# Block attention and a squared-ReLU FFN on one core: two turns fewer on TensorE, four sums in place of five, shared reciprocals, and an order of tasks that is written down

## The chip, the core and the metric

The kernel runs on one core of a Trainium2 chip. The core has TensorE (PE, the matmul engine, with its weight loads as PEld), VectorE (DVE), ScalarE (ACT), GpSimd (POOL) and SyncE (SP, which issues nearly all DMAs); they work side by side, each takes its own instructions strictly in order, and semaphores tie them together. The metric is the device time of one execution in microseconds, the median of several runs. A profile shows one further execution, whose span is a little shorter than a run's time.

## The reference, cut to what matters

Four batches of 768 tokens with eight heads of 64 go through local attention, and the 3072 tokens that come out through an FFN with weights of 512 x 2048 and 2048 x 512. All is in float32.

```python
k_sum = k.reshape(B, H, nb, 32, D).max(axis=3)        # nb = 24 block keys
v_sum = v.reshape(B, H, nb, 32, D).mean(axis=3)
scores_l = where(|i - j| < 16, scale * q @ k.T, -1e9)
scores_s = scale * q @ k_sum.T + log(32)
a = exp(concat - max);  a = a / (sum(a) + 1e-9)
x = a @ concat(v, v_sum)                              # to (3072, 512)
out = (max(x @ w_in, 0) ** 2) @ w_out
```

## The kernel before

**Tasks and queues.** The program is built from some 2400 named tasks. Each has an engine, a cost, a key (when it is due), the tasks it comes after, and the buffers it takes and uses. `Plan.order` (lines 234 to 355) is a planner that goes through time with these costs and keys and yields one list; the order of a task on its engine is its place in that list. Keys are moved by hand in a table `NUDGE`, and the first loads on SP are in a list `FIRST`.

**Attention.** The tokens are 48 groups of 64, taken in pairs. A group g has these tasks: QL, LV, LS load queries, values and block sums; KL, KM load keys (four blocks for each batch) and take their block maxima on DVE; KC and KW make copies of keys; S is the scores on PE, 16 matmuls in two halves, a second sixteen at the start adding the mask by PE (groups below `PE_MASKS = 8`; the scores' maximum is then X on DVE, line 945), while from group 8 on DVE masks and takes the maximum in M and Mb (line 913); E is four exponentials on ACT with their sums (line 976, one per pair of heads); R is the reciprocal on DVE (`inverse`, lines 988 to 995: an add with an accumulated by-product, then the reciprocal); N normalises, on DVE or on ACT (`NORMAL_BY`); T turns the weights. If `TURN_BY` gives a pair to PE, T is four transposes by PE and A a copy on ACT; if it gives it to DVE, T is a transpose by DVE within 32 x 32 squares, TW stores the pair to memory and TR_0 to TR_3 fetch it back in the turned layout, all on SP's queue. V is the visit: the pair's products with the values on PE, next to the scores of a later pair. XH and XL split the result into a high and a low part. All matmuls of the FFN are three products of such parts.

**FFN.** A unit is 512 tokens. Units 0 and 1 run plainly: for each of 16 slices f, FI (12 matmuls of 128 x 512, into the hidden slice), RL, SQ and GH on ACT, GL on DVE, FO (12 matmuls back; for f = 0 and 1 of unit 0 both come in halves a and b, FO in halves of six). Weights for it are loaded by WL, and split by WM and WH on ACT and WR, WJ and WW on DVE: the FFN's task FI0_f needs WH and WW of weight 0 and slice f (from f = 3 on both weights share a task, WW3). The remaining 2048 tokens are two super-units s, each of four blocks, multiplied in the seven-product scheme: `mixed` (lines 1777 to 1968) does the seven products with w_in, eight hidden blocks p at a time (SP tasks on PE, 56 per s), `products` (lines 1539 to 1667) the seven with w_out (FP, 56 per s), product j over its eight p after another. The sums of the weights (RC, SC, SH, SL, WS, and with i for w_in) are done on DVE and ACT meanwhile.

**The sums of the second products.** For every p four squared hidden parts `first`, `second`, `diff`, `last` are there. Of the seven left factors, five take a DVE addition of 128 x 512: TA1 and TB1 in `mixed` (lines 1884 to 1891 and 1937, 1938), and one each for j = 2, 5 and 6 (TA, lines 1578 to 1599). GH on ACT (line 1601) and GL on DVE (line 1605) then split the factor, and FP multiplies it with a loaded chunk of the weights (CL). A product runs in a bank of `o` over its eight p; after the eighth, U1 (ACT, line 1647), C11, U2, U3, C22, C21, C12 (DVE) take the banks out.

**Dummies.** Y tasks (`warm`, line 555) are pairs of dummy matmuls on PE that fill the start, 16 before the first scores and 8 more behind them.

## Time and profile before

| | |
|---|---|
| median of 3 runs | 567.49 us (567.41 to 567.75) |
| span of the profiled execution | 566.3 us |
| instructions in it | 11867 |
| PE busy | 557.6 us, 98% |
| weight loads busy | 459.4 us, 81% |
| DVE busy | 470.2 us, 83% |
| ACT busy | 373.9 us, 66% |
| POOL busy | 36.7 us, 6% |

The profile is read from the whole to the place: the totals of the engines, the chain of work that ended last (each step followed back to what released it), the waits of one engine by what released them, the chain or an engine's instructions in order of time, and the instructions grouped by line. Busy times of neighbours on one engine can overlap, since instructions are pipelined; the distance between two starts is then what one of them costs.

### The profile page before, as it was taken

To read this page: it belongs to the slowest core of one execution; us is meant where nothing else is said; L and a number is where in the kernel's file an instruction comes from. 1 tells how busy PE (TensorE), PEld (TensorE's weight loads), DVE (VectorE), ACT (ScalarE), POOL (GpSimd) and SP (SyncE) were. 2 spreads that over 40 slices of the span, in tenths; PEclk is the share of its full clock that TensorE was granted. 3 is DMA by queue.
4 is the path that set the end of the run, shared out by engine and by line. 5 is a ranking of instruction groups with operands and counts; after the bars stand their busy time and mean duration, and the time that the engine had idled before them with its cause. 6 is when DMAs were issued, how large, how long until landed. Compare 5 with 4: busy or idle time off the path is not lost.

```text
span 566.3 us, 11867 instructions
## 1 busy us (share of the span) xinstructions
PE 557.6 (98%) x3955; PEld 459.4 (81%) x3955; DVE 470.2 (83%) x1191; ACT 373.9 (66%) x968; POOL 36.7 (6%) x88
## 2 busy tenths in 40 slices
PE   8899999999999999999999999999999999999997
PEld 8688888888888888888888888888888888888885
DVE  4999999988799998999978889997493556868864
ACT  3899899878877987786336688847374532554442
POOL 4300000012001130000000200000000000000000
PEclk9999999999999999999999999999999999999999
DMA  8998999999989999899877989897975666767672
GB/s 314 354 371 306 364 328 383 290 289 370 341 272 323 322 341 371 301 293 393 298 211 236 292 247 284 274 281 239 281 224 159 194 190 194 193 197 230 191 234 96
DMA packets 86953, 156.75 MB, mean 277 GB/s; under 512 B 9011, under 2 KB 30837, under 8 KB 86893
## 3 DMA queue, kind: packets, MB, share of 16 engines
q1 hardware_dynamic: 85741, 152.95, 82.8%
q0 software_dynamic: 1152, 3.05, 3.2%
q8 instruction: 32, 0.52, 0.4%
q14 instruction: 28, 0.23, 0.1%
HBM read 111.66 MB, written 47.94 MB: 282 GB/s over the span
## 4 chain that ended last, share of the span: by engine, by line
PE 95%; ACT 2%; DVE 2%; issue 0%; POOL 0%; DVEq 0%; POOLq 0%; ACTq 0%
PE o L1620 23%; PE o L1322 16%; PE h L1296 15%; PE o L1844 14%; PE sz L1844 8%; PE att L1620 4%; PE x L1099 4%; PE att L840 3%; PE sa L1844 3%; PE att L1844 2%; PE warm L559 2%; ACT qvpa_lent L978 1%; PE t L1028 1%; DVE small L933 0%; PE o L840 0%; PE h_1a L1296 0%
## 5 line engine op out<-in xcount | busy, mean ns | idle before, releaser
L1602 ACT CAST gh<-g 128x512 fp32r<-128x512 f32 x112 | 69.2, 621 | 53.1 <-PE o L1620 22.7
L1620 PE MATMUL o<-gh,w 128*128 128x512 f32 x384 | 103.2, 391 | 0.0
L1607 DVE TENSOR_TENSOR gl<-g,gh 128x512 fp32r<-128x512 f32 x112 | 76.0, 685 | 21.1 <-ACT gh L1602 20.0
L1620 PEld LDWEIGHTS o<-gh,w 128*128 128x128 f32 x384 | 71.7, 188 | 14.9
L1296 PE MATMUL h<-xh,w 128*128 128x512 f32 x240 | 74.5, 391 | 0.0
L1881 ACT ACTIVATE g<-g 128x512 f32<-128x512 f32 x60 | 37.8, 632 | 49.4 <-DVE g L1877 49.3
L1322 PE MATMUL o<-w,gh 128*128 128x512 f32 x240 | 62.3, 395 | 0.0
L978 ACT ACTIVATE p<-p,small 128x118 f32<-128x118 f32 x160 | 61.8, 391 | 0.7 <-DVE small L915 0.7
L1620 PE MATMUL o<-gl,w 128*128 128x512 f32 x192 | 59.2, 389 | 0.0
L1296 PEld LDWEIGHTS h<-xh,w 128*128 128x128 f32 x240 | 44.7, 188 | 9.5 <-ACT rl_0b L1305 0.3
L1322 PEld LDWEIGHTS o<-w,gh 128*128 128x128 f32 x240 | 44.1, 188 | 9.4 <-ACT rl L1306 0.2
L1296 PE MATMUL h<-xl,w 128*128 128x512 f32 x120 | 46.7, 389 | 0.0
L1620 PEld LDWEIGHTS o<-gl,w 128*128 128x128 f32 x192 | 36.0, 188 | 7.6
L1844 PE MATMUL o<-w,w 128*128 128x512 f32 x160 | 40.5, 389 | 0.0
L1844 PEld LDWEIGHTS o<-w,w 128*128 128x128 f32 x160 | 30.0, 188 | 6.2
L915 DVE CUSTOM_DVE_ANT_0 p<-att,mask 128x118 f32<-128x118 f32 x152 | 32.9, 274 | 2.1 <-PE att L840 2.0
L1844 PE MATMUL sz<-xh,w 128*128 128x512 f32 x128 | 34.3, 390 | 0.0
L1322 PE MATMUL o<-w,gl 128*128 128x512 f32 x120 | 33.6, 389 | 0.0
L1597 DVE TENSOR_TENSOR g<-g 128x512 f32<-128x512 f32 x48 | 32.6, 684 | 0.2
L1877 DVE CUSTOM_DVE_ANT_0 g<-sz,g 128x512 f32<-128x512 f32 x32 | 22.0, 687 | 12.0 <-ACT g L1864 6.9
L978 ACT ACTIVATION_READ_ACCUMULATOR p<-p,small 128x1 f32 x160 | 31.2, 195 | 0.0
L1844 PE MATMUL o<-xh,w 128*128 128x512 f32 x112 | 30.1, 390 | 0.0
(197 smaller groups left out, 1093.9 us busy)
## 6 DMA issues: line engine op xcount, KB each, us to landing
raw<-wW SPq DMA_DIRECT2D x32, 512.0 KB, 7.7
w<-scr_t SPq DMA_DIRECT2D x64, 256.0 KB, 3.0
w<-scr_s SPq DMA_DIRECT2D x64, 256.0 KB, 3.0
w<-scr_a SPq DMA_DIRECT2D x48, 256.0 KB, 3.3
w<-scr_i SPq DMA_DIRECT2D x44, 256.0 KB, 3.1
turn<-a SPq DMA_DIRECT2D x17, 512.0 KB, 4.7
scr_t<-ci SPq DMA_DIRECT2D x16, 512.0 KB, 8.1
v<-vS SPq DMA_DIRECT2D x34, 192.0 KB, 3.5
```

The lines of the kernel that those rows point to most:

```text
L915: nc.vector.tensor_tensor_reduce(out=pr.tile[:, j, :KEYS], in0=score_at(g, 0, j), in1=mask_of(g)[0], scale=-SCALE, scalar=-NEG, op0=ALU.ad ...
L978: nc.scalar.activation(x, score_tile(g, p % parts)[:, p] if by_pe else x, AF.Exp, bias=nm.tile[:, p : p + 1], scale=SCALE if by_pe else -1 ...
L1099: nc.tensor.matmul(x_of(i)[h % 2 * D : (h % 2 + 1) * D, h // 2, :], lhsT=v_bufs[g].tile[:KEYS, h * D : (h + 1) * D], rhs=av[:KEYS, 2 * c : ...
L1296: nc.tensor.matmul(cut(h), lhsT=lhs.tile[:, k // 2, k % 2 * P : (k % 2 + 1) * P], rhs=rhs[:, k, c0 : c0 + n], start=(i == 0), stop=(i == 3 ...
L1322: nc.tensor.matmul(o_of(o, t).rearrange("p (h c) -> p h c", h=2), lhsT=terms[i][0].tile[:, (t - t0) * P : (t - t0 + 1) * P], rhs=terms[i][ ...
L1597: lambda x=x, ins=ins, op=op: nc.vector.tensor_tensor(out=x.tile, in0=ins[0].tile, in1=ins[1].tile, op=op),
L1602: f"GH{s}_{n}", "ACT", 0.54, lambda x=x, gh=gh: nc.scalar.copy(out=gh.tile, in_=x.tile), due - GH_LEAD, ready,
L1607: lambda x=x, gh=gh, gl=gl: nc.vector.tensor_tensor(out=gl.tile, in0=x.tile, in1=gh.tile.bitcast(F32), op=ALU.subtract),
L1620: nc.tensor.matmul(o.tile[:, d, c], lhsT=chunk.tile[:, w * HALF + d * P : w * HALF + (d + 1) * P], rhs=y.tile[:, c], start=begins and w == ...
L1844: nc.tensor.matmul(o.tile, lhsT=lhs(w, k), rhs=y[k], start=begins and i == 0, stop=i == 5, skip_group_check=not begins,)
L1877: lambda: nc.vector._custom_dve(TENSOR_ADD_SAT, out=to.tile, in0=o.tile, in1=x.tile, s0=HUGE, s1=0.0), key, deps,
L1881: f"G{name}_{s}", "ACT", 0.57, lambda: nc.scalar.activation(to.tile, to.tile, AF.Square), key + 0.7, [t], use=[to]
```

## The change

- **Who turns.** `TURN_BY` gives PE the pairs 0 to 4 and 13 in place of 0, 1, 2, 3, 5, 8 and 12. Groups 10, 11, 16, 17, 24 and 25 go to DVE, groups 8, 9, 26 and 27 to PE: two turns fewer by PE, two more by DVE, one store and four fetches more on SP.
- **Who masks.** `MASK_BY` replaces `PE_MASKS`: group 5 is masked by DVE (M5, M5b), not by PE.
- **Reciprocals.** From group 10 on one R serves a pair (48 become 29), after the exponentials of both groups; the accumulated by-product of its add is gone. N of both groups comes after it.
- **Who normalises.** ACT normalises 17 groups in place of 21, DVE the other 31.
- **Four sums.** T1 and T3 stand behind the product j = 0 of their p, T2 and T4 at j = 2; TA1, TB1 and the three TA are gone: 80 additions become 64. The products run j = 0 for the eight p, then j = 1 and 2 in turn for each p, then j = 3 to 6 as before (`in_turn`).
- **The order.** The planner, `NUDGE` and `FIRST` go; `SEQUENCE` names all tasks in one order for all engines, and `order` walks it and gives out buffers. Dummies: 22 in place of 24, five of them between the first scores S0_0 and the second S0_1 in place of nine. On DVE the four key maxima KM0_0 to KM0_3 stand ahead of X0_0 (before: KM0_0 KM0_1 X0_0 KM0_2 KM0_3 X0_1). On SP the first loads are KL0_0 QL0 KL0_1 KL0_2 KL0_3 WL0_0 QL1 QL3 FV0_0 (before: KL0_0 KL0_1 QL0 KL0_2 KL0_3 QL1 QL2 WL0_0 FV0_0).
- The costs (second number of a task) and keys that change have no effect but on which place of a ring a buffer gets.

PE's order around the first FFN products, worked out from both programs:

```
before: ... T5 FI0_0a V4 V5 T6 T7 S8 V6 V7 FI0_1a S9 FI0_0b FI0_1b FO0_0a FI0_2
        FO0_1a FI0_3 FO0_0b FI0_4 FO0_1b S10 FO0_2 FI0_5 FO0_3 T10 FI0_6 T11 FO0_4 V9 ...
after:  ... T5 T6 S9 V2 V6 T7 FI0_0a V5 V4 FI0_1a V7 T8 FO0_0a S10 FI0_1b FO0_1a T9 FI0_0b FI0_2
        FI0_3 FO0_0b FO0_1b FI0_4 FO0_2 FI0_5 FO0_3 V9 FO0_4 FI0_6 ...
```

What stands on DVE ahead of WW0_2 in the new order and did not before: N8, N9, R9, WR1_2, WJ1_2, and M5, M5b in place of X5. On ACT ahead of WH0_2: E8_3, the four E9, A8, WM1_2, KW11, RL0_1b and GH0_1a.

The diff, cut:

```diff
-PE_MASKS = 8
+MASK_BY = 'PPPPPDPPDD'
-WARM, COLD, AGAIN = 16, 10, 8
+WARM, COLD, AGAIN = 14, 13, 8
-NORMAL_BY = 'DDDDDDDDDDDDDAADDDDDAADDADAAAADADDADAADADAAAAADAA'
+NORMAL_BY = 'DDDDDDDDDDDAAADDADDADDAADDDDDDDDDDAADAAAADADADAA'
-TURN_BY = 'PPPPDPDDPDDDPDDDDDDDDDDD'
+TURN_BY = 'PPPPPDDDDDDDDPDDDDDDDDDD'
+SEQUENCE = """
+ident KL0_0 KM0_0 QL0 KL0_1 KM0_1 KL0_2 KL0_3 WL0_0 QL1 QL3 FV0_0 QL2 C3 C1 FV0_2 QL4 FV0_4 FV0_1 FV0_5 FV0_3 WL0_1 Y0 Y1 Y2 WL1_0 Y3 mask-15 C4 LV0
+Y4 Y5 QL5 Y6 QL6 QL7 LV1 LV3 Y7 Y8 C0 unscale table Y9 Y10 Y11 KM0_2 KM0_3 Y12 mask0 S0_0 X0_0 E0_0 means Y13 Y14 Y15 C5 E0_2 Y16 Y17 S0_1 KC0 WM0_0
...
+E43_3 XPL1_0_1 GL0_7' CL0_10 G21_4_0 GH0_8' M42b FP0_6_0 CL0_18 FP0_7_0 E42_3 GL0_8' FP0_8_0 T10_6 KW45 GH0_16 GL0_16 E42_2 CL0_11 CL0_19 CL0_12
+GH0_9' GL0_9' V41 U1_0 T20_3 GH0_17 E43_2 R43 N43 G12_7_0 FP0_16_0 QL46 LV42 N42 KC45 XF39_1 GL0_17 GH0_10' FP0_9_0 GH0_18 QL47 T42 T43 TW43 GL0_10'
...
     def order(self):
...
+        started = [named.pop(name) for name in SEQUENCE]
...
-        by_pe = g < PE_MASKS
+        by_pe = MASK_BY[g] == "P"
...
-            x, ins, op = (
-                (first, None, None), (second, None, None), (first, (last, first), ALU.add), (last, None, None),
-                (diff, None, None), (second, (second, first), ALU.subtract), (diff, (first, diff), ALU.add),
-            )[j]
+            x = (first, second, None, diff, first, second, last)[j]
+            ready = [t_G[s, p, k] for k in ((0,), (1,), (), ("T3",), ("T1",), ("T4",), (3,))[j]]
...
+                less("T2", x, last, first, due - GH_LEAD - 1.3, [t_G[s, p, 3], t_G[s, p, "T1"]], [both] * (p % 2 == 0))
+                less("T4", second, second, x, due - GH_LEAD - 0.7, [t_G[s, p, "T2"], t_G[s, p, "in", 1]])
...
+            if j == 0:
+                at = due + NQ * PRODUCT_STEP[s] - GH_LEAD
+                less("T1", first, diff, first, at + SUM_LEAD[0], [t_l, t_G[s, p, 2]])
+                less("T3", diff, last, diff, at + SUM_LEAD[1], [t_G[s, p, "T1"], t_G[s, p, 3]])
...
-                    t_G[s, p, 3] = less(f"TA1_{p}", last, last, diff, key + 1.5, [t, self.g22])
-                    t_G[s, p, 2] = less(f"TB1_{p}", diff, diff, first, key + 2.5, [t_G[s, p, 3], t_G[s, p, 0]])
+                    t_G[s, p, 3] = self.g22
...
-    def in_turn(js, start, step):
-        return [(j, p, start + (i * NQ + p) * step) for i, j in enumerate(js) for p in range(NQ)]
+    def in_turn(start, step):
+        turns = [(0, p) for p in range(NQ)] + [(j, p) for p in range(NQ) for j in (1, 2)] + [(j, p) for j in range(3, PRODUCTS) for p in range(NQ)]
+        return [(j, p, start + i * step) for i, (j, p) in enumerate(turns)]
```

## Rows read from the trace of the kernel before

**Rows 1.** The page: busy time and share of each engine; the last chain by engine.

```profile
PE 557.6 (98%) x3955; PEld 459.4 (81%) x3955; DVE 470.2 (83%) x1191; ACT 373.9 (66%) x968; POOL 36.7 (6%) x88
PE 95%; ACT 2%; DVE 2%; issue 0%; POOL 0%; DVEq 0%; POOLq 0%; ACTq 0%
```

**Rows 2.** Waits of PE: line, releaser, us in total, times, longest us.

```profile
PE t L1028 <- DVE qvpa_lent L999: 1.6, 3, 0.8
PE warm L559 <- POOL ident masks.py:199: 1.4, 1, 1.4
```

**Rows 3.** Windows: us and instructions busy per engine, granted clock, DMA share, GB/s.

```profile
0.00:20.00 20.00, 17.57 (x265) 14.98 (x266) 12.44 (x34) 9.03 (x35) 8.99 (x45) 1.00 0.92 327
20.00:40.00 20.00, 18.07 (x322) 15.17 (x323) 18.89 (x59) 19.53 (x72) 4.39 (x13) 1.00 1.01 364
```

**Rows 4.** Chains of waits of 33 to 60 and 118 to 130 us: start, us, piece.

```profile
42.28 2.85 PE h L1296 x12
45.14 1.36 PE o L1322 x6
...
54.66 0.97 PE att L840 x32
55.62 2.99 PE o L1322 x12
...
123.54 0.44 PE t L1028 x4
123.98 2.77 PE o L1322 x12
```

**Rows 5.** DVE in order of time: start, us, instruction, idle before and releaser.

```profile
3.88 0.95 DVE L595 TENSOR_REDUCE kb<-kb 128x24 f32<-128x768 f32 x1 [3.88 <-DMA kb<-kT]
5.12 0.95 DVE L595 TENSOR_REDUCE kb<-kb 128x24 f32<-128x768 f32 x1 [0.28 <-DMA kb<-kT]
...
11.28 0.40 DVE L933 TENSOR_REDUCE small<-o 128x2 f32<-128x236 f32 x1 [0.84 <-PE o L840]
...
41.38 0.66 DVE L1246 TENSOR_TENSOR w<-t,w 128x512 fp32r<-128x512 f32 x1
```

**Rows 6.** ACT in order of time, at the cast of weight 0_2.

```profile
39.46 0.69 ACT L1239 CAST w<-t 128x512 fp32r<-128x512 f32 x1
```

**Rows 7.** Instructions by line, DVE, then ACT: busy us, mean ns, idle before.

```profile
L1597 DVE TENSOR_TENSOR g<-g 128x512 f32<-128x512 f32 x48 | 32.6, 684 | 0.2
L1887 DVE TENSOR_TENSOR g<-g 128x512 f32<-128x512 f32 x32 | 22.0, 686 | 2.6 <-ACT g L1881 2.1
...
L993 DVE RECIPROCAL small<-small 128x4 f32<-128x4 f32 x48 | 8.6, 178 | 1.7
...
L978 ACT ACTIVATE p<-p,small 128x118 f32<-128x118 f32 x160 | 61.8, 391 | 0.7 <-DVE small L915 0.7
```

**Rows 8.** DVE in order of time among the products of super-unit 1.

```profile
494.02 0.68 DVE L1597 TENSOR_TENSOR g<-g 128x512 f32<-128x512 f32 x1
494.62 0.68 DVE L1607 TENSOR_TENSOR gl<-g,gh 128x512 fp32r<-128x512 f32 x1
```

**Rows 9.** Groups 14 and 15: DVE turn, SP fetches, PE visit; such fetches overall.

```profile
110.73 0.70 DVE L1057 STREAM_TRANSPOSE a<-p 128x512 f32<-128x512 f32 x1
...
115.68 3.68 SPq L1077 DMA_DIRECT2D a<-turn  x4
...
127.65 1.15 PE L1099 MATMUL x<-a,v 118*64 118x64 f32 x32
...
a<-turn SPq DMA_DIRECT2D x34, 128.0 KB, 4.1
```

**Rows 10.** PE, then ACT in order of time around U1 of super-unit 1.

```profile
496.26 0.62 PE L1620 MATMUL o<-gl,w 128*128 128x512 f32 x2
498.07 1.07 PE L1620 MATMUL o<-gh,w 128*128 128x512 f32 x4
...
496.99 1.01 ACT L1648 COPY u<-o 128x1024 f32<-128x1024 f32 x1
```

More of the change, by code (lines that the diff above doesn't have):

```diff
@@ L234, in order @@
     def order(self):
+        named = {}
         for t in self.tasks:
-            x = NUDGE.get(f"{t.engine}.{t.name}", 0.0)
-            t.key = round(t.key + x, 4)
-            t.begin = round(t.begin + x * (t.engine == "SP"), 4)
-        then = {t: [] for t in self.tasks}
-        for t in self.tasks:
-            t.wait = len(set(t.after))
-            for a in set(t.after):
-                then[a].append(t)
-            for b in t.take + t.use:
-                b.left = len(b.users)
-        ready = {}
-        for t in self.tasks:
-            ready.setdefault(t.engine, [])
-            if not t.wait:
-                ready[t.engine].append(t)
-        free = dict.fromkeys(ready, 0.0)
-        free["SP"] = 0.8
-        events, n, pipe, landed = [], 0, 0.0, []
-        started, narrow, grain, held = [], False, 0.0, dict(DVE=0.0, POOL=0.0)
-        for t in self.tasks:
+            name = t.name
+            while name in named:
+                name += "'"
+            named[name] = t
+            for b in t.take + t.use:
+                b.left, b.end = len(b.users), -1e9
             kind = t.name.rstrip("0123456789_ab")
@@ L602, in batch_k @@
             t_KL.append(t)
-            t_K[b].append(add(f"KM{b}_{p}", "DVE", 0.85, lambda p=p: top(p), key + 0.1 * p, [t]))
+            t_K[b].append(add(f"KM{b}_{p}", "DVE", 0.862, lambda p=p: top(p), key + 0.1 * p, [t]))
     t_VS, vs_bufs = {}, {}
@@ L676, in first_sums @@
         own = len(tail) % 4 == 0
-        t_VS[0] = [add("VS0", "DVE", 0.85, gather, -53, [last], take=[vs] * own, use=[out_ps] + [vs] * (not own))]
+        t_VS[0] = [add("VS0", "DVE", 1.1, gather, -53, [last], take=[vs] * own, use=[out_ps] + [vs] * (not own))]
     scr_v = {
@@ L1017, in softmax @@
         elif NORMAL_BY[g] == "A":
-            t_n = add(f"N{g}", "ACT", 1.2, normal_by_act, due - 10, [t_r], use=[pr, nm])
+            t_n = add(f"N{g}", "ACT", 1.145, normal_by_act, due - 10, [t_r], use=[pr, nm])
         else:
@@ L1172, in visit @@
             t_f = [
-                add(f"XF{g}_{k}", "ACT", 0.3, lambda k=k: whole(k), due + 0.5 - X_LEAD, [t_v], take=[x[k]] * new, use=[x_ps] + [x[k]] * (not new))
+                add(f"XF{g}_{k}", "ACT", 0.268, lambda k=k: whole(k), due + 0.5 - X_LEAD, [t_v], take=[x[k]] * new, use=[x_ps] + [x[k]] * (not new))
                 for k in range(2)
@@ L1445, in combine @@
             ))
-        t2 = add(f"SC{p}", engine, 2.9 if by_pool else 1.5, add_up, due + 2.6, t1, use=xs)
+        t2 = add(f"SC{p}", engine, 2.9 if by_pool else 1.45, add_up, due + 2.6, t1, use=xs)
         t5 = []
@@ L1868, in plus @@
             return add(
-                f"{name}_{s}", "DVE", 0.615, lambda: nc.vector.tensor_tensor(out=to.tile, in0=o.tile, in1=x.tile, op=ALU.add), key, deps,
+                f"{name}_{s}", "DVE", 0.605, lambda: nc.vector.tensor_tensor(out=to.tile, in0=o.tile, in1=x.tile, op=ALU.add), key, deps,
                 use=[o, x, to],
@@ L1881, in sum_squared @@
                 f"G{name}_{s}", "ACT", 0.57, lambda: nc.scalar.activation(to.tile, to.tile, AF.Square), key + 0.7, [t], use=[to]
-            )
-        def less(name, to, a, b, key, deps):
-            engine, tensor, cost = ("DVE", nc.vector, 0.615) if s or LESS_BY == "D" else ("POOL", nc.gpsimd, 1.25)
-            return add(
-                f"{name}_{s}", engine, cost, lambda: tensor.tensor_tensor(out=to.tile, in0=a.tile, in1=b.tile, op=ALU.subtract), key, deps,
-                use=[a, b, to],
             )
```

397 lines of the change are left out of this document (232 added, 165 removed), and 4 rows, old and new, of the table NUDGE.

## The prediction, made before the changed kernel was run

> **What bounds the kernel now.** I read the page's totals first. PE is busy for 557.6 us of 566.3, DVE for 470.2, ACT for 373.9, and the chain that ended last is 95% PE [rows 1]. Then the waits of PE: 1.4 us before its first product, and after that the largest is a turn that waits for a normalisation by DVE, 1.6 us in three places [rows 2]. The windows say where PE idles: it is busy for 17.57 of the first 20 us and for 18.07 of the next 20, where ACT is busy for 19.53, DVE for 18.89 and the DMA engines all the time [rows 3]. In the chain in order of time, the PE pieces follow on one another from FI0_2 on, the first full FFN product, at 42.28 us: 42.28 + 2.85 is where the next begins, and so on [rows 4]. So there are two regimes. Up to about 42 us four engines feed one another; after it PE runs without a gap, and only work taken off PE, or a PE made to wait, moves the end. The profiled span is 566.3 us and the median of the runs 567.49, so 1.2 us lie around the span; I sum in the span and add 1.2.
>
> **Work of PE after FI0_2.** The sum hangs on one point: when FI0_2 issues, and what PE has still to do then. Before, 566.3 - 42.28 = 524.0 us remain. The new order puts three things ahead of FI0_2 that stood behind it: the product FO0_1a, six matmuls or 1.36 us; the scores S10, 0.97 us, with some 0.27 that the twelve matmuls behind them take longer (2.99 against twice 1.36); and two turns [rows 4]. A turn by PE costs 0.44 us and 0.05 that the block behind it takes longer, 0.49 [rows 4]. Behind FI0_2 stood six turns (groups 10, 11, 16, 17, 24, 25), and two are left (26, 27): 4 x 0.49 = 1.96. Together 1.36 + 1.24 + 1.96 = 4.56 us less remain, 519.5. The break-even is therefore an FI0_2 at 42.28 + 4.56 = 46.8 us. Of the 4.56, only the 0.98 of the two turns that leave PE altogether is gone for good; the rest is work brought forward, and pays only if PE's idle time ahead of FI0_2 takes it.
>
> **When FI0_2 issues.** Ahead of it PE gains two turns, S10 and FO0_1a, 0.98 + 1.24 + 1.36 = 3.58 us. It loses the sixteen mask products of group 5 (DVE masks it now; half of S10's 32 products of like shape is 0.49, so 0 to 0.5 less [rows 4]) and two groups of dummy products, counted at nothing. With the idle time of before, FI0_2 comes at 42.28 + 3.58 = 45.9 us. The idle of the first 40 us is 2.43 + 1.93 - 1.4 ahead of the first product [rows 2, 3], 3.0 us; with none of it, and without the masks, FI0_2 comes at 42.4.
> How much idle goes? DVE's start of before shows the cause. The first two key blocks landed 1.24 us apart (their maxima start at 3.88 and 5.12), yet the second row maximum ran at 11.28, after waiting 0.84 us for PE's scores [rows 5], because the maxima of key blocks three and four stood behind the first row maximum, and those scores behind both. In the new order all four key maxima stand ahead of it. At 1.24 us a block the fourth lands near 3.88 + 3.7 = 7.6 us; with its maximum of 0.95 and the 0.84 for the scores that gives 9.4 for the second row maximum, 1.9 us earlier at best; at worst 0, if the new queue order or the full DMA engines hold the key blocks back.
> The other two engines set floors. On DVE the last weight step that FI0_2 needs ended at 41.38 + 0.66 = 42.0 [rows 5]. Ahead of it the new order has N8, N9, two half steps of weight 1_2, and masks for group 5 in place of its maximum: four steps of at most that 0.66 each, 2.0 to 2.6: 44.0 to 44.6, or 42.1 with the earlier start. On ACT the last weight cast ended at 39.46 + 0.69 = 40.2 [rows 6]; ahead of it come five more exponentials of 0.39 [rows 7] and five more steps, none above the 0.69 of that cast, some 2 us: 44.2, or 42.3 with the earlier start. PE 42.4 to 45.9, DVE from 42.1, ACT from 42.3: as the engines wait for each other in order, I take 44.0, above every floor and below the case without any gain. End: 44.0 + 519.5 = 563.5.
>
> **What is off the path.** The block sums: five additions become four, 80 instructions (48 + 32 of 684 to 686 ns [rows 7]) become 64. An addition and the step behind it stand 0.60 us apart [rows 8], so 16 x 0.60 = 9.6 us less DVE. The reciprocals: 48 become 29, at 0.178 us each [rows 7] 3.4 us less, and their sums go with them. Two more turns on DVE (0.70 [rows 9]) and four more normalised groups (at most 0.66) give back 1.4 + 2.6. DVE's total falls by some 9 us, and ACT's by the four groups. I count all that at zero: after 42 us PE waits for neither. Its cover is PE's own gapless queue; if that cover goes, the saving shows (rival C).
>
> **What is added, and may wait.** (1) The products for j = 1 and 2 now take turns, so the bank that U1 empties is wanted one product after FP_7. Before, U1 on ACT started 0.11 us after that product's last matmuls (496.26 + 0.62), ran 1.01, and ended 0.07 ahead of the next product but one at 498.07 [rows 10]. The margin is 0.07; an exponential of 0.39 [rows 7] ahead of U1 would cost 0.3. It comes once per super-unit: 0 to 0.6. (2) The sums T2 and T4 stand between gl steps of j = 1 and 2, and part of T1 and T3 with them. Two DVE steps of 0.60 meet one product of 1.36: it fits, with 0 to 1.0 where more steps than that meet it. (3) A shared reciprocal makes the first group's N wait for the second group's exponentials; behind it on DVE stand weight steps and gl. The pair is turned and visited together anyway, so 0, at worst one exponential of 0.39. (4) The written order moves loads on SP's queue; a load that lands late shows as a PE wait, and the nearest row is 1.6 in three places [rows 2]: 0 to 0.9. I take 0.3 for all four, near the lower ends, since DVE and ACT get lighter: span 563.8, run **565.0**.
>
> **A turn moved to DVE.** Groups 10/11, 16/17 and 24/25 leave PE for DVE, store and fetch; 8/9 and 26/27 come back. The thinnest pair that I found: second turn at 110.73, four fetches issued from 115.68 to 119.36, 4.1 us to landing, so 123.5; its visit reads them at 127.65 [rows 9]. That is 16.9 us where PE takes 0.49, with 4.2 us to spare. PE runs in order, so a late fetch stops the visit and all FFN products behind it.
> The Trainium skill speaks against the move: VectorE: DVE Perf Modes, Rules for kernel authors, wants TensorE for a 128x128 transpose if PSUM will do as the destination, and its section The three transpose paths says that DVE turns only blocks of 32x32. By that rule the moved pair is a loss, which is rival B; the trace agrees that the way over DVE is long, but shows PE as the engine without a gap.
>
> **Rivals.** *A, no gain in the start:* FI0_2 at 45.9 or later, because ACT and the DMA engines were full and earlier keys only wait elsewhere. 45.9 + 519.5 + 0.3 + 1.2 = 566.9; with another 0.8 of waits 567.7. For: ACT's 19.53 of 20 us [rows 3]. Against: DVE's wait before 11.28 was due to order alone. Chance 0.16.
> *B, slower:* the visits of the moved pairs (V11, V17, V25) wait for their fetches. It decides once the second turn, or SP's queue behind it, slips more than 4.2 us against PE; three visits that are each 1.5 us later than that cost 4.5: 569.5. For: the DMA engines are full in the stretch before, and PE arrives earlier. Against: 4.2 us is the thinnest case. Chance 0.08.
> *C, more gain:* DVE, not PE, is the limit, and its 9 us show: 567.5 - 9 = 558.5. Against it: six matmuls take 1.36 us and twelve 2.77 to 2.85, 80 us apart [rows 4]; PE issues at its own pace. Chance 0.03.
> Beside C stands the Trainium skill, Perfetto Trace Analysis, Identifying the Most-Contended Engine: it judges TensorE's headroom by MFU and by its weight loads, not by matmul busy time. The loads are 81% here, below DVE's 83% [rows 1]; the trace disagrees, as the pieces without a gap show.
> That the change doesn't do what it says (a written order that makes engines wait where the planner's did not) lies in terms (1) to (4): all at their upper ends are 2.9 us, with the forecast's start 567.6.
>
> **How the numbers follow.** Forecast 0.73, A 0.16, B 0.08, C 0.03. The forecast's own spread: FI0_2 between 42.4 and 45.2, waits between 0 and 1.0. Low: 42.4 + 519.5 + 0 + 1.2 = 563.1, and 0.4 less for the dummy products counted at nothing: 562.7. High: A's 567.7. Left out are B, C and the ends, under 0.2. A measurement tells about 0.2% from no change, 1.1 us: faster is below 566.4, slower above 568.6. Most of the forecast and nothing of A lies below 566.4: faster 0.74 with C; same 0.16; slower 0.10.
>
> **What would show it.** Right: FI0_2 issues at 43 to 45 us, the second row maximum at 9.4 to 10.5, PE without a gap from FI0_2 on, two PE turns after it where there were six, DVE's busy total below 465. Wrong: FI0_2 beyond 46; PE waiting at a visit's values for a DMA; a wait two products after FP_7; gaps in the products. The forecast fails most easily at FI0_2, since each microsecond there is one at the end.

## The result, and the profile after

The changed kernel takes 571.76 us (median of 5 runs, 570.87 to 573.1), the kernel before 567.75 on the same chip: a ratio of 1.0074, with an interval of 1.0061 to 1.0087. It is slower by 0.7%, clear of the noise, against a forecast of 565.0 and a range that ended at 567.7. The profiled execution, the longest of its runs, took 573.1 with a span of 571.4.

The page of the changed kernel: totals of the engines, DMA share in tenths and rate in 40 slices, and the last chain by engine.

```profile
PE 559.3 (98%) x3927; PEld 458.2 (80%) x3927; DVE 459.1 (80%) x1101; ACT 365.6 (64%) x950; POOL 37.6 (7%) x88
...
DMA  8999699998998999989798998678966767676763
GB/s 300 338 382 383 231 338 341 306 304 308 307 356 290 277 337 370 349 261 353 270 280 301 329 320 278 195 239 248 305 207 190 194 191 231 192 193 193 229 185 139
...
PE 65%; DVE 14%; DMA 12%; ACT 4%; issue 2%; SPq 2%; ACTq 0%; DVEq 0%
```

Against [rows 1], DVE did fall by 11 us and ACT by 8, as meant. PE has 28 instructions fewer, and yet 1.7 us more busy time. The chain that ended last is PE's for 65% where it was for 95%, and transfers have 12% of it. In the waits of PE there is more than a start [rows 2]:

```profile
PE vps L699 <- issue: 1.9, 1, 1.9
PE x L1157 <- DMA a<-turn: 1.5, 2, 0.8
PE warm L596 <- POOL ident masks.py:199: 1.4, 1, 1.4
PE h L1354 <- ACT rl L1363: 1.1, 2, 0.7
PE t L1086 <- DVE qvpa_lent L1057: 0.7, 2, 0.4
PE h L1354 <- DVE w L1304: 0.6, 1, 0.6
```

PE in order of time shows where: rows of the changed kernel that have an idle time before them (in brackets, with what ended it).

```profile
19.32 0.41 PE L699 MATMUL vps<-fv_lent,means 128*24 128x128 f32 x6 [1.93 <-issue]
...
46.08 0.62 PE L1354 MATMUL h<-xh,w 128*128 128x512 f32 x2
...
116.52 0.50 PE L1354 MATMUL h<-xh,w 128*128 128x512 f32 x1 [0.56 <-DVE w L1304]
...
139.22 0.73 PE L1354 MATMUL h<-xh,w 128*128 128x512 f32 x2 [0.35 <-ACT rl L1363]
...
153.56 0.65 PE L1157 MATMUL x<-a,v 118*64 118x64 f32 x15 [0.85 <-DMA a<-turn]
...
177.04 0.74 PE L1354 MATMUL h<-xh,w 128*128 128x512 f32 x2 [0.74 <-ACT rl L1363]
...
206.90 0.82 PE L1157 MATMUL x<-a,v 118*64 118x64 f32 x21 [0.69 <-DMA a<-turn]
...
567.14 0.50 PE L1687 MATMUL att<-gh,w 128*128 128x256 f32 x2 [0.52 <-DVE u L1624]
```

The row at 46.08 is FI0_2, whose start in the same view of before is 42.12 (the chain of [rows 4] has 42.28). After it stand six idle times, 3.71 us together; before had one, of 0.20. I cut the span at two landmarks, FI0_2 and the first product of super-unit 0 (`sa`):

| | before | changed | difference |
|---|---|---|---|
| FI0_2 | 42.12 | 46.08 | +3.96 |
| FI0_2 to `sa` | 193.70 | 193.78 | +0.08 |
| `sa` to the end of the span | 330.48 | 331.54 | +1.06 |
| span | 566.3 | 571.4 | +5.1 |

The middle row is the finding that needs explaining. By the pieces of PE, 4.1 us of work had left that stretch (4.56 in the prediction, which took 0.27 of S10's neighbours and the 0.05 beside each turn twice). It took as long as before: 3.2 us came back as the idle times above, and 1.0 in matmuls that took longer (PE is busy for 190.6 us in it, where 193.7 less 4.1 leaves 189.6). So there are two questions: what delayed FI0_2, and who holds the stretch behind it.

### The profile page after: what moved, and what is told of

Same layout as the page of the kernel before. It is cut to its first block, busy times and chain, and to the rows that moved or that the text cites. A ratio compares the mean times of both kernels' runs of the same rounds, so it can differ in the third digit from the quotient of the medians.

```text
span 571.4 us, 11676 instructions
## 1 busy us (share of the span) xinstructions
PE 559.3 (98%) x3927; PEld 458.2 (80%) x3927; DVE 459.1 (80%) x1101; ACT 365.6 (64%) x950; POOL 37.6 (7%) x88
## 4 chain that ended last, share of the span: by engine, by line
PE 65%; DVE 14%; DMA 12%; ACT 4%; issue 2%; SPq 2%; ACTq 0%; DVEq 0%
PE o L1687 23%; PE o L1911 14%; PE sz L1911 8%; PE att L1687 4%; PE o L1380 4%; DMA raw<-wW 4%; DMA kb<-kT 3%; PE sa L1911 3%; PE h L1354 2%; PE x L1157 2%; DMA a<-turn 2%; PE att L1911 2%; PE att L878 2%; DVE kb L632 1%; DMA out<-os 1%
## 5 line engine op out<-in xcount | busy, mean ns | idle before, releaser
L1665 ACT CAST gh<-g 128x512 fp32r<-128x512 f32 x96 | 59.3, 620 | 57.8 <-PE o L1687 33.4
L1670 DVE TENSOR_TENSOR gl<-g,gh 128x512 fp32r<-128x512 f32 x96 | 65.6, 688 | 27.1 <-ACT gh L1665 25.8
L1948 ACT ACTIVATE g<-g 128x512 f32<-128x512 f32 x60 | 35.6, 623 | 14.8 <-DVE g L1944 14.8
L1911 PEld LDWEIGHTS sz<-xh,w 128*128 128x128 f32 x128 | 23.9, 188 | 5.2 <-DVE g L1944 0.2
```

The costliest lines, as they stand in the source:

```text
L1665: f"GH{s}_{n}", "ACT", 0.52, lambda x=x, gh=gh: nc.scalar.copy(out=gh.tile, in_=x.tile), due - GH_LEAD, ready,
L1670: lambda x=x, gh=gh, gl=gl: nc.vector.tensor_tensor(out=gl.tile, in0=x.tile, in1=gh.tile.bitcast(F32), op=ALU.subtract),
L1911: nc.tensor.matmul(o.tile, lhsT=lhs(w, k), rhs=y[k], start=begins and i == 0, stop=i == 5, skip_group_check=not begins,)
L1948: f"G{name}_{s}", "ACT", 0.57, lambda: nc.scalar.activation(to.tile, to.tile, AF.Square), key + 0.7, [t], use=[to]
```

## Experiments on the start

The stop of 1.93 us came after PE's 218th matmul, in VM0_4, and "issue" says that the profile shows nothing that PE waited for. In before PE stopped for 0.21 us, also after its 218th matmul, which there was a score. Behind the stop the granted clock fell (windows of the changed kernel; the last three columns are clock, DMA share, GB/s):

```profile
18.00:20.00 2.00, 0.68 (x18) 0.47 (x22) 0.36 (x2) 1.89 (x7) 0.00 (x0) 0.99 1.06 385
20.00:22.00 2.00, 2.00 (x32) 1.70 (x25) 1.58 (x5) 0.00 (x0) 0.81 (x2) 0.50 1.01 337
22.00:24.00 2.00, 2.00 (x28) 1.51 (x28) 1.29 (x5) 1.64 (x8) 0.00 (x0) 0.65 0.91 322
24.00:26.00 2.00, 2.00 (x53) 1.71 (x50) 1.93 (x12) 2.00 (x9) 0.86 (x3) 1.00 0.96 333
```

0.50 is the lower level, 1.2 GHz; PE had been busy for 0.68 of the 2 us before.

**The changed kernel once more.**

> The changed kernel once more, nothing altered. In its first profile PE stood still for 1.93 us after its 218th matmul, at 17.4 us, with no releaser that the profile knows, and the kernel before stood still for 0.21 us after its own 218th matmul at the same time. Theory F (PE waits there for its next instructions): again exactly after matmul 218, with a length of its own between 0.2 and 2 us, and FI0_2 moves with it (44.4 to 46.2 us). Rival V (the matmul waits for a late block of values): the same place in the code, 1.9 us again. The waits in the FFN stretch should return at the same visits and FI products, 3 to 4 us in sum.

571.41 us, span 569.7. The stop came again behind the 218th matmul, 1.27 us long (18.78), with no fall of the clock, and FI0_2 issued at 44.57, near the forecast's 44.0. The stretch took 193.54. So the length of the stop varies from one execution to the next. The stop was 0.66 us shorter and FI0_2 came 1.5 us earlier, so the clock may have the rest of that; but a start 1.5 us earlier did not bring the forecast nearer: with FI0_2 at 44.57 the forecast's own sum gives a span of 564.4.

**Values or instructions.** VM0_4 multiplies loaded values; either they came late, or the instructions did.

```diff
-... VM0_4 ... S4_0 ...
+... S4_0 VM0_4 ...
```

> The changed kernel with one task moved on PE: the last sums of values VM0_4 stand behind the scores S4_0 instead of ahead of them. Theory F: PE again stands still after its 218th matmul, which now lies inside S4_0, for 0.2 to 2 us, and VM0_4 runs through. Rival V: S4_0 runs through and the wait shows inside VM0_4, shorter by the 0.9 us that S4_0 takes, about 1 us.

573.08 us. VM0_4 now waited for nothing, and PE stopped inside S4_0, behind the 217th matmul:

```profile
17.58 0.43 PE L878 MATMUL o<-kb,qvpa_lent 64*64 64x118 f32 x8 [0.17 <-issue]
...
19.40 0.33 PE L878 MATMUL o<-mask,unscale 64*64 64x118 f32 x4 [1.33 <-issue]
```

Where it comes, the stop keeps to the number of instructions, not to the task: not the values. It does not always come: e_mend, m_dve, m_act, m_dma and u_r below, with the changed kernel's order up to there, have none behind the 218th matmul.

**Weight loads out of the way.** If the full DMA engines delayed PE's instructions, fewer loads there should help.

```diff
-... WL0_1 Y0 Y1 Y2 WL1_0 ... LV3 ...
+... Y0 Y1 Y2 ... LV3 WL0_1 WL1_0 ...
```

> The changed kernel with the weight loads WL0_1 and WL1_0 (512 KB each, issued at 11.4 us) moved on SP's queue behind LV3, where the kernel before has them later too. If the stop after matmul 218 is long because these transfers are ahead of the instructions' own on the DMA engines, it shrinks from 1.9 to below 1 us and the granted clock stays at 1.0; if it has nothing to do with them, it stays between 1 and 2 us.

576.21 us. Two stops, after 264 and 296 matmuls, and longer ones:

```profile
22.13 0.63 PE L878 MATMUL o<-kb,qvpa_lent 64*64 64x118 f32 x16 [2.69 <-issue]
...
24.60 0.67 PE L878 MATMUL o<-kb,qvpa_lent 64*64 64x118 f32 x8 [1.23 <-issue]
```

The stops got no shorter, so that explanation has no support; but the two loads were only moved, and this is one execution. The cause of the stop's length stays open.

**The start of before, the rest changed.**

```diff
-SEQUENCE up to FI0_4: the changed order
+SEQUENCE up to FI0_4: the order of the kernel before
```

> The changed kernel with the start of the kernel before: up to the fourth FFN slice all engines take the order of the kernel before (key maxima, first loads, 24 dummies, group 5 masked by PE), from there the changed order; turns, sums and reciprocals stay changed. Theory S (the start is a cost of its own that adds to the rest): FI0_2 at 42.3 to 43 us in place of 46.1, the waits after it stay at 3 to 4 us, so 571.8 - 3.4 + 2.6 (work that the changed order had brought ahead of FI0_2 stands behind it again) = about 570 to 571. Rival C (the FFN stretch is bound by DVE, ACT and the weight loads, not by when PE gets there): an earlier PE only waits longer, the waits after FI0_2 grow by 2 us or more, and the time is 572 or above.

574.31 us, ratio 1.0121 (1.0101 to 1.0141): slower still, although FI0_2 issued at 41.73, where before has it. The stretch took 198.8 us, with seven idle times (117.97: 1.17; 178.38: 0.74). `sa` comes at 240.5; it came at 239.9 and 238.1 above. The test is weaker than it looks, since this order puts 46 of PE's instructions behind FI0_2 again (FO0_1a, S10 and two turns by PE, 1.36 + 0.97 + 0.88 = 3.2 us): of the 4.3 us of earlier start 1.1 could have shown at `sa`, and none did. Five runs in which PE has the changed kernel's work in the stretch say it better: with FI0_2 at 43.57 (m_act), 43.77 (e_mend), 44.11 (m_dve), 44.57 (a_again) and 46.08, `sa` comes at 237.4, 239.4, 240.2, 238.1 and 239.9, in no order. So the start is not the main point.

## Experiments on the parts

**The order alone.** Before's order written out in the changed program, with none of the parts, is the control (h_none); then the shared reciprocals alone (h_r), the changed turns alone (h_turn), and all but the four sums (h_all5).

```diff
 h_none: TURN_BY, NORMAL_BY, MASK_BY, WARM, five sums and SEQUENCE as before
 h_r:    h_none, and  paired = g >= FIRST_S
 h_turn: h_none, and  -TURN_BY = 'PPPPDPDDPDDDPDDDDDDDDDDD'
                      +TURN_BY = 'PPPPPDDDDDDDDPDDDDDDDDDD'
```

> The control: the order of the kernel before, written out as the list of the changed kernel, with none of the parts (five sums, a reciprocal for each group, the turns and masks of before). Writing an order down should cost nothing by itself: 567 to 568.2 us. If it comes out at 570 or more, the way in which the changed program walks its list (the places of buffers, or which instruction carries which wait) costs, and not the order in it.

> The order of the kernel before with the shared reciprocals alone: from group 10 on the first group's reciprocal is gone and its normalisation stands behind the pair's one. Theory O (the written order costs, the parts don't): 567 to 568.2. Rival P (the parts cost: the normalisation that waits for the second group delays what is queued behind it on DVE and ACT): 569 or more, with PE waiting at FI for ACT or at visits for DVE.

> The order of the kernel before with the changed turns alone: groups 10, 11, 16, 17, 24 and 25 turned by DVE in the places where PE turned them, with store and fetches behind, and 8, 9, 26 and 27 by PE. By my step on the turns PE has 0.98 us less: 566.3 to 567.5, and no wait at V11, V17 or V25 above 0.3 us. Rival P: PE waits for fetches at these visits or for the two more turns at the start of the FFN, 569 or more.

> The order of the kernel before with all parts but the four sums: turns, shared reciprocals, masks of group 5 by DVE, 17 groups normalised by ACT. Theory O: 566 to 568, four us below the changed kernel, since only the written order and the sums are missing. Rival P: 570 or more, and the sum of what h_r and h_turn show says which part.

569.47 (ratio 1.0027), 571.98 (1.0081), 580.2 (1.0211) and 581.9 us (1.0247). The control is 1.5 us above before, with one idle time of 0.54; why, beyond other places of buffers, I did not find out. The shared reciprocals cost 2.5 us against it where I had 0, at worst 0.39: turns wait for ACT (0.68 at 68.29), FI for ACT (0.43 at 152.74). The turns cost 10.7, with visits and turns that wait:

```profile
144.15 1.14 PE L1160 MATMUL x<-a,v 118*64 118x64 f32 x24 [2.77 <-ACT gh L1370]
...
201.55 1.18 PE L1089 MATMUL t<-ident,p 128*128 128x128 f32 x4 [2.78 <-ACT p L1067]
```

The visit at 144.15 is V17, of a moved pair. Its fetches were issued from 139.50 to 140.81, so they, and not the step of ACT that the profile names, may be what it waited for. These tasks were put in at places between their neighbours, not in an order made for them. So h_turn and h_all5 bound a part's price only together with its place.

**The parts taken out of the changed order.**

```diff
 u_r:
-        paired = g >= FIRST_S
+        paired = False            (each R behind its own group's E)
 u_turn:
-TURN_BY = 'PPPPPDDDDDDDDPDDDDDDDDDD'
+TURN_BY = 'PPPPPPDDPDDDPPDDDDDDDDDD'
```

> The changed kernel with a reciprocal for each group again, each right behind its group's last exponential and the group's normalisation behind it; order otherwise as changed. Theory R (the shared reciprocal holds back the first group's normalisation, and what stands behind it on ACT and DVE): PE's waits in the FFN stretch shrink by 1 to 2.5 us, 569.3 to 570.8. Rival: the order was written around the shared ones, DVE gets 19 x 0.33 us more, and the time is 571.5 to 573.

> The changed kernel with the three pairs 10/11, 16/17 and 24/25 turned by PE again, where their DVE turns stood; 8/9 and 26/27 stay with PE. PE has six turns more: at 0.49 each 2.9 us, if PE is the bound in that stretch, less the 0.7 that it waited for the fetches of 24/25: about 574. If PE is not the bound there (it waits for DVE and ACT in any case, and two fetch queues fewer help SP), the turns hide in its waits: 571.8 or below.

581.53 (1.0238) and 585.28 us (1.0305): both slower than the changed kernel too, by some 10 and 14 us. In u_turn PE waits for N on DVE (4.04 at 65.36, 3.27 at 193.04). The parts are fitted to their order, in both directions; none can be priced alone in this way.

**The four sums alone**, in before, with its planner. The products take turns as in the changed kernel.

```diff
-            x, ins, op = ((first, None, None), ... (diff, (first, diff), ALU.add))[j]
+            x = (first, second, None, diff, first, second, last)[j]
+            (T2, T4 at j = 2; T1, T3 behind j = 0; TA1, TB1 gone)
```

> The kernel before with the four sums and the products in turn alone, ordered by its planner; PE's order is that of before up to the ninth product of super-unit 0. By my steps on the sums: 9.6 us less on DVE, nothing of it on the path, a cost of 0 to 0.6 at U1 and 0 to 1.0 in the alternating products: 567.3 to 569. Rival C (DVE is the limit): 565 or below. Rival W (U1 and the sums make PE wait): 570 or above, with PE's waits in the products of j = 1 and 2.

568.77 us, ratio 1.0013 (1.0004 to 1.0023), no wait of PE in the products. DVE's saving there is off the path and the alternation costs 0.7 us (0.2 to 1.3), as forecast. The time from `sa` to the end of the span is 0.5 us longer than in before, with no idle time of PE: that is the other half of the 1.06 in the table above, beside the wait of 0.52.

## Experiments on the stretch behind FI0_2

Of the waits in that stretch the profile names ACT's rl, DVE's w and the fetches. **First I mended four of them, and the tail, by their order.** In before FP1_55_3 stands ahead of C12_1_True; the changed order writes the addition in between, and the last half product waits for it.

```diff
-FP1_55_2 C12_1_True FP1_55_3
+FP1_55_2 FP1_55_3 C12_1_True
 also: RL1_0 ahead of E21_3; GL1_5 ahead of two sums; WW14 ahead of SCi1_1
```

> The changed kernel with four places of its written order mended, nothing else: the last half product is written ahead of the addition of its other half; RL1_0 stands ahead of the exponential E21_3 on ACT; GL1_5 stands behind SC5 but ahead of two sums of weights on DVE; WW14 stands ahead of SCi1_1 on DVE. Theory O (in the changed kernel PE waits because single steps of DVE and ACT stand behind others that nobody waits for): the waits of PE of 0.52 at the last product, 0.35 at FI1_1, 0.74 at FI1_7 and 0.56 to 0.76 at FI0_14 go, and the time falls by about 2.2 us to 569.6. Rival L (DVE and ACT are behind as a whole there): the waits come back at the next FFN product, and only the 0.5 at the end is gained, 571.2.

572.38 us, 1.0072 (1.0051 to 1.0093): nothing gained. The four waits and the tail's 0.52 were gone, and others had come (e_mend, PE):

```profile
102.03 0.50 PE L1354 MATMUL h<-xh,w 128*128 128x512 f32 x1 [1.21 <-DVE w L1304]
...
153.52 0.69 PE L1157 MATMUL x<-a,v 118*64 118x64 f32 x16 [1.34 <-DMA a<-turn]
...
175.34 0.63 PE L878 MATMUL att<-kw,q 64*64 64x118 f32 x16 [0.77 <-ACT kw L903]
```

The stretch took 195.6. So I took a resource as a whole to be behind there, and my theory was DVE and ACT, on whose steps PE waited. **Then I lightened one resource at a time**: DVE (gl on half of its columns), ACT (relu and square on half), the transfers (queries by half, and adding transfers of 4 rows in place of 96), and all three. Each of these kernels leaves out a part of the work.

```diff
 m_dve:
-  tensor_tensor(out=cut(gl), in0=cut(r), in1=cut(gh), op=ALU.subtract)
+  tensor_tensor(out=some(gl), in0=some(r), in1=some(gh), op=ALU.subtract)
 m_act:
-  activation(cut(r), cut(h), AF.Relu); activation(cut(r), cut(r), AF.Square)
+  activation(some(r), some(h), AF.Relu); activation(some(r), some(r), AF.Square)
 m_dma:
-  dma_start(out=q.tile, in_=qW[g])
+  dma_start(out=q.tile[:, : NPAIR // few(g)], in_=qW[g][:, : NPAIR // few(g)])
-  gpsimd.dma_start(out=to, in_=x, accum_op=ALU.add)
+  gpsimd.dma_start(out=to[:4], in_=x[:4], accum_op=ALU.add)
```

> The changed kernel, with DVE lighter: from FI0_6 on the step gl of every full unit is done for half of its columns (256 of 512; the second products use the written half twice, so their count is the same and the values are wrong). In the stretch from FI0_2 to the first product of the second super-unit some 26 such steps save 0.26 us each, 6.8 us of DVE. The stretch took 193.8 us in the changed kernel and 193.5 in its repeat, and the products' work without any wait is about 189.6 (193.7 before, less the 4.1 that left it). If DVE as a whole holds it: 190.5 or less, PE waits in it under 1 us, total 567 to 569. If the waits hang on ACT or on loads: 193 or more, total 571.

> The changed kernel, with ACT lighter: from FI0_6 on relu and square of every full unit are done for half of their columns, and the cast and gl read that half twice (values wrong, all other work the same). Some 26 units save 0.4 us each, 10.5 us of ACT, in the stretch from FI0_2 to the second super-unit. If ACT as a whole holds it: 190.5 us or less (193.5 to 193.8 without), total 567 to 569. If DVE or loads hold it: 193 or more, total 571.

> The changed kernel, with fewer bytes moved: from group 8 on the query loads bring half of a group (the scores use that half twice), and the adding transfers on POOL's queue for the block sums of the later batches touch 4 rows instead of 96 (values wrong, as many instructions on every engine). Of the 62 MB in the stretch some 4 go, and most of the POOL queue's 9.5% of the DMA engines' time. If the DMA engines as a whole hold the stretch: 190.5 us or less (193.5 to 193.8 without), total 567 to 569. If DVE or ACT hold it: 193 or more.

> The three lightenings at once (gl half, relu and square half, fewer bytes). If the waits come from engines that are too full in turn, so that each alone only uncovers the next: the stretch falls to 190.5 us or less here although no single one brought it there, total 566 to 568. If they come from the written order (steps that stand behind a step that waits, however short each is): still 192.5 or more.

| | FI0_2 | FI0_2 to `sa` | PE idle in it | time us | ratio to before |
|---|---|---|---|---|---|
| changed kernel | 46.08 | 193.78 | 3.19 | 571.76 | 1.0074 |
| m_dve | 44.11 | 196.07 | 4.43 | 573.04 | 1.0075 |
| m_act | 43.57 | 193.86 | 3.21 | 571.99 | 1.0073 |
| m_dma | 44.23 | 189.58 | 0 | 567.12 | 0.9997 |
| m_all | 46.22 | 189.26 | 0 | 566.53 | 0.9980 |

Lighter DVE or ACT gives nothing, fewer bytes take every wait of PE out of the stretch and bring it to the 189.6 that its work needs. FI0_2 and the stretch are of one execution each, but the times of five to eight executions say the same. My theory fell. The waits of PE, first m_act, then m_dma, down to the start's and the tail's:

```profile
PE h L1365 <- DVE w L1304: 1.5, 2, 1.2
PE h L1365 <- ACT rl L1374: 0.8, 1, 0.8
```

```profile
PE warm L596 <- POOL ident masks.py:199: 1.4, 1, 1.4
PE o L881 <- DVE kb L632: 1.2, 3, 0.5
PE t L1089 <- DVE qvpa_lent L1060: 0.7, 2, 0.4
PE o L881 <- POOL kb L894: 0.6, 1, 0.6
PE att L1690 <- DVE u L1627: 0.5, 1, 0.5
```

The last chain of m_dma is PE's again, as in before (95%):

```profile
PE 94%; DVE 3%; DMA 1%; ACT 1%; SPq 0%; issue 0%; ACTq 0%
```

How a transfer becomes a wait for another engine is plainest in m_dve: DVE stood 5.70 us for a weight load, and PE 2.76 us for the weight that DVE then made.

```profile
101.50 0.69 DVE L1283 TENSOR_SCALAR raw<-raw 128x1024 uint32<-128x1024 uint32 x1 [5.70 <-DMA raw<-wW]
...
104.38 0.50 PE L1359 MATMUL h<-xh,w 128*128 128x512 f32 x1 [2.76 <-DVE w L1304]
```

The waits of DVE in 46 to 240 us, the changed kernel:

```profile
DVE ci L1528 <- DMA out<-os: 2.4, 1, 2.4
DVE raw L1283 <- DMA raw<-wW: 1.7, 1, 1.7
DVE cs L1464 <- DMA scr_t<-ci: 1.7, 1, 1.7
...
DVE kb L632 <- DMA kb<-kT: 0.9, 1, 0.9
```

DVE stands for transfers four times, 6.7 us, where before stood 2.4; in m_dma it is 0.8 at scr_t and 0.3 at raw. What is behind it in DVE's queue, gl and w among it, comes later; ACT's rl waited 11.7 us for gl in this stretch (7.2 in m_dma, 3.5 in before); and PE's h waits for rl. This is read from the sums. Followed one by one, neither of PE's two waits for rl comes right behind such a wait for gl: before the one at 139.22 ACT had stood 1.58 us for a mask step of DVE, before the one at 177.04 for PE's own visit. The two visits, 1.5 of the 3.2 us, wait for a transfer directly; the last fetch of the one at 153.56 was issued at 145.41, some 8 us before, where the landings known of before took 3.1 to 6.9. DVE's steps themselves are no shorter in m_dma (gl 685 ns against 688), and POOL issues as many instructions, so it is the transfers and not a shared engine. Which of the two cuts in bytes counts was not separated.

**Where the transfers fall behind.** Up to `sa` the changed kernel had moved 77.8 MB in 239.9 us, at 324 GB/s, and before 78.4 MB in 235.8, at 332. Not more bytes: idle DMA engines. By an estimate from these rates, the 77.8 MB would have been moved by 234.1 us at the 332 GB/s of before, close to the 233.8 at which m_dma reaches `sa`. So DMA engines as full as those of before would not have cost the 4 us. They moved less per us, and what held them back, or whether that only follows from the waits, is the question. The changed kernel in windows of 2 us (the last two columns are DMA share and GB/s):

```profile
62.00:64.00 2.00, 2.00 (x10) 1.65 (x10) 2.00 (x4) 2.00 (x10) 0.00 (x0) 1.00 0.87 349
64.00:66.00 2.00, 2.00 (x35) 1.49 (x37) 1.97 (x5) 1.82 (x8) 0.00 (x0) 1.00 0.06 23
66.00:68.00 2.00, 2.00 (x51) 1.70 (x43) 1.97 (x4) 1.97 (x4) 0.54 (x1) 1.00 0.04 8
68.00:70.00 2.00, 2.00 (x11) 1.63 (x10) 2.00 (x7) 1.97 (x5) 0.00 (x0) 1.00 0.37 152
```

and SP's queue there, in order of time, then its largest wait between 40 and 110 us:

```profile
57.69 0.43 SPq L1277 DMA_DIRECT2D raw<-wW  x1
68.48 0.33 SPq L1130 DMA_DIRECT2D turn<-a  x1
68.85 0.43 SPq L1277 DMA_DIRECT2D raw<-wW  x1
69.32 0.72 SPq L742 DMA_DIRECT2D vt_lent<-vT  x1
```

```profile
SPq L1130 <- DVE small L961: 10.4, 1, 10.4
```

Before has such waits at stores too (42 to 240 us):

```profile
SPq L1072 <- DVE a L1057: 16.8, 5, 7.0
```

The store at 68.48 is TW11, of the first pair that the change gives to DVE. SP stood at it for 10.4 us until DVE had turned the pair (the second turn, named a<-p, ends at 68.45; the line names a step of DVE next to it), and the weight loads WL0_10 and following, which need nothing, stood behind it; from 64 to 68 the DMA engines had hardly anything to move. In before the same ten microseconds, 60 to 70, have a share of 1.09, in the changed kernel 0.47. Later ones are thinner too: 110 to 120 has 0.80 against 0.99, 170 to 180 0.81 against 1.07. But SP's standing at stores is not new: over 42 to 240 us, whatever it stood there for, it is 20.5 us in before, 26.4 in the changed kernel and 29.5 in m_dma, where PE waits for nothing in the stretch.

**The store moved behind loads**, in two tries.

```diff
 m_sp:
-WL1_11 TW11 WL0_10 FT1_2 QL14 WL1_10 WL0_15 TR11_3
+WL1_11 WL0_10 QL14 WL1_10 WL0_15 TW11 FT1_2 TR11_3
 m_sp2:
+WL1_11 WL0_10 WL1_10 WL0_15 TW11 FT1_2 QL14 WL0_12 WL1_12 LV11 TR11_3   and the tail of e_mend
```

> The changed kernel with one store moved in the written order: TW11, the store of the first pair that the change moved to DVE (10 and 11), goes behind WL0_10, QL14, WL1_10 and WL0_15 on SP's queue, and FT1_2 behind it. In the changed kernel SP stood at that store from 58.1 to 68.5 us for DVE's second turn of the pair, four weight loads, a query load and a key load behind it, and the DMA engines were busy for 0.47 of 60 to 70 us (before: 1.09). If that hole sets the later waits: SP issues the weight loads at 58 to 60, the DMA share of 60:70 is above 0.75, the stretch from FI0_2 to the second super-unit falls from 193.5-193.8 to 190-191.5, total 567.5 to 569. If the loads could not go earlier (their buffers are taken), or the later waits come from bytes added elsewhere: the hole stays or the stretch stays at 193 or more, total 571. If the fetches of the pair now come behind the loads and its visit V11 waits: a wait of 0.5 or more for a DMA there.

> The changed kernel with SP's queue reordered around the first moved store, and the tail mended. In the changed kernel the DMA engines were idle from 63.7 to 69.2 us (share 0.06 and 0.04 in 64:66 and 66:68). In m_sp the queue stood at QL14 instead (7.2 us, its buffer was still read by the scores) and the hole stayed. Now only loads that need no buffer of others go ahead of the store TW11: WL0_10, WL1_10 and WL0_15; behind it QL14, FT1_2, WL0_12 and WL1_12 go ahead of the pair's fetches. FP1_55_3 goes ahead of C12_1_True (worth 0.5 in the four mends). If the hole sets the later waits: DMA share above 0.75 in 60:70, FI0_2 to the second super-unit 190 to 191.5, total 567.5 to 569 (571.5 less 0.5 and 2.3 to 3.5). If the bytes as such hold the stretch, or other holes further on do: 193 or more, total 571. If the fetches now come too late for V11: a wait of 0.5 or more there.

m_sp: 573.8 us (1.0103). The queue stood at QL14 instead, 7.2 us, whose buffer the scores were still reading, and the share of 60:70 was 0.61 and of 70:80 0.72. The hole had moved and the stretch took 196.2: a miss that says to look at each load's buffer. m_sp2: 570.87 us, 1.0051 (1.0032 to 1.0070). Its windows:

```profile
60.00:70.00 10.00, 10.00 (x100) 8.15 (x99) 9.93 (x22) 9.73 (x25) 0.58 (x1) 1.00 0.93 359
110.00:120.00 10.00, 9.43 (x42) 7.47 (x41) 9.17 (x26) 8.09 (x27) 1.69 (x2) 1.00 0.80 233
170.00:180.00 10.00, 9.26 (x95) 7.33 (x94) 9.48 (x36) 8.67 (x25) 0.31 (x1) 1.00 0.83 296
```

The first hole is filled, the stretch takes 192.6 with 2.07 us of PE idle, and the tail's wait is gone. That is 0.9 to 1.2 of the 2.3 to 3.5 that I had expected of the hole alone, and even this is not clear of the noise: `sa` comes at 237.8, where a_again, with a share of 0.64 in 60:70, has 238.1, and the interval of the ratio overlaps that of the changed kernel (1.0061 to 1.0087), with the tail's 0.5 us in the difference. So the hole is seen, and that it is a cause of the waits is not shown. The later holes are as before the mend, and stores of turns are among what SP stands at there (12.7 us in seven waits for DVE's turn between 40 and 240). That these carry the waits was not tried. In m_dma the holes stay (0.57 in 60:70) and PE waits for nothing in the stretch, so the holes by themselves do not make it wait.

## Why the prediction was wrong, point by point

**When FI0_2 issues: the mechanism right, one cost unseen.** The four key maxima did move ahead of X0_0, and the time taken was 44.0; it was 44.57 in a_again, 44.11 in m_dve, 43.57 in m_act and 44.23 in m_dma, inside 43 to 45. Where PE had no stop behind the 218th matmul it came at 43.6 to 44.2 (m_dve, m_act, m_dma, u_r, e_mend), with stops of 1.3 to 1.7 us at 44.6 to 45.2 (a_again, u_turn, m_sp2), and with stops of 1.8 or 1.9 us and the clock falling behind them at 46.1 to 46.5 (the changed kernel, m_all, m_sp). In e_vm, whose order differs there, it came at 46.2 with 1.33. The second row maximum came at 10.65 (11.28 in [rows 5]) and not at 9.4 to 10.5: the second key maximum on DVE waited 1.90 us for its key block, which now stands behind QL0 on SP. In the profiled execution the stop behind the 218th matmul grew from 0.21 to 1.93 us and the clock fell behind it, and FI0_2 came at 46.08. No row of before shows a stop of that length, and it varies: between two executions of the changed kernel the stop differs by 0.66 us and FI0_2 by 1.5.

**Work of PE after FI0_2: right as work, 0.47 too much.** Only two turns are left, and m_dma's 189.58 against 193.70 shows the 4.1 us. That kernel ends with a span of 564.9, where the sum had 563.8: 0.2 of the difference is FI0_2's, 0.5 the tail's and 0.5 what was counted twice; 0.3 had been put down for waits, which goes off; and the 0.2 left is FI0_2 of before, taken as 42.28 for 42.12. The 1.2 us around the span were a pair of unlike executions: in the runs here time less span is about 1.7, which puts the profiled execution of before at 568.0, 0.5 us above its median.

**"After 42 us PE waits for neither": the step that failed.** I took PE's gapless queue as proof that nothing else was near its limit, and counted what DVE and ACT lose at zero. In the changed kernel PE waits for 3.2 us between FI0_2 and `sa`. The runs agree on DVE and ACT (m_dve, m_act; b_four for the sums). What stood next to PE were the transfers: with fewer bytes the stretch falls from 193.78 to 189.58 and PE waits for nothing in it. [Rows 3] had them at 1.01 from 20 to 40 us, and I read that for the start alone; the same view of before goes on at 0.86 to 1.09 up to 240 us. With both that full, 4.1 us less of PE's work pays only as far as the transfers keep up, and here they fell behind: `sa` came between 237.4 and 240.5 in the changed kernel, a_again, e_start, e_vm, e_mend, m_dve and m_act, with FI0_2 anywhere from 41.7 to 46.2, and at 242.7 and 243.4 in m_sp and e_wl, which moved loads. Before had 235.8, and the sum gives 233.1 (44.0 and 193.70, less 4.56). What in the change made the transfers late stays open. The Trainium skill, Perfetto Trace Analysis, Identifying the Most-Contended Engine, which I set aside for what it says of weight loads, also judges the DMA engines, by the rate from memory and not by their busy share. Here the rate would have left more room than the share: 332 GB/s up to `sa` in before, between 277 and 383 in windows of 10 us, where the changed kernel reaches 399 in one (30 to 40 us).

**Term (4), loads on SP's queue, 0 to 0.9: mis-sized, and looked for in only one place.** I looked for a late load as a wait of PE for a DMA. Such waits are 1.5 of PE's 3.2 us; the rest are for DVE and ACT, and DVE stood at loads. Fewer bytes, on SP's queue and in the adding transfers together, give back 4.2 us in the stretch (193.78 less 189.58); what SP's loads alone are worth was not separated.

**A turn moved to DVE.** I checked that the fetches of the moved pairs land in time, but not what is queued behind their store. That store held SP for 10.4 us, at a price that m_sp2 does not show. Rival B named "SP's queue behind it" and priced only the visits: two waits, 0.85 at V19 and 0.69 at V25, of which V25 alone is a moved pair. Its sign was right; its path is at most a small part of it here, though in h_turn V17, a moved pair, waited 2.77 us. The Trainium skill's VectorE: DVE Perf Modes, Rules for kernel authors, which wants TensorE for such a turn, is not contradicted by this trace, with the 10.4 us beside it; u_turn, which put three pairs back in the same order, can't confirm it.

**Term (3), the shared reciprocal, 0 to 0.39.** In before's order it costs 2.5 us (h_r against h_none); within the changed order its price stays open.

**Terms (1) and (2).** Right: no wait two products after FP_7 and none in the products of b_four. Unforeseen was the written place of C12_1_True, 0.52 us at the tail, which e_mend and m_sp2 took away.

**Rivals.** A's times, 566.9 to 567.7, were missed by 4 us, though FI0_2 came beyond its 45.9 in the profiled execution; B's 569.5 lies nearest. C is refuted: 11 us less of DVE did not show.

**What stays open:** why the stop of PE varies; why h_none is 1.5 us above before; what made the transfers late, the holes or something else; whether the queries or the adding transfers count in m_dma; and what each part costs in an order of its own. No run here was faster than before with its full work; m_dma and m_all move fewer bytes.

## What to carry to other kernels

A busiest engine without a gap does not say that the next resource is far: before counting work removed from it as gained, read the DMA share over the whole stretch, and if it is near 1 too, ask what the change does to the transfers. On an in-order DMA queue a store that waits for a result holds every load behind it, so look at what is queued behind a moved store and at the idle DMA time that it makes (seen here; its price was not), and put ahead of it only loads whose buffers are free. When mending single waits brings others, lighten one resource at a time: it names the resource in a few runs, though not why it is late.
